# One fused kernel, one hand-written step list: the order of 808 steps is changed and 54 steps change engine

## The chip, the cores and the metric

The kernel runs on one core of one Trainium2 chip. The metric is the device time of one execution in microseconds (us). Five engines work side by side, each through its own list of instructions in order: TensorE (PE, matrix products into PSUM), VectorE (DVE), ScalarE (ACT), GpSimd (POOL), and SyncE (SP), which issues every DMA transfer of this kernel on one queue.

## The reference, cut to what matters

`x` is `A_q`, 2048 rows of 512 numbers in bf16.

```python
n  = layernorm(x)
ks = sum over t of shift(k, t) * shift_k[:, t]     # 4 taps
kv = ks * v
y  = causal_convolution(kv, ssm_k) + kv * ssm_D    # by FFT of length 4096
h  = x + n * y
m  = layernorm(h)
x1 = m + mixed(gelu(layernorm(m) @ w1)) @ w2       # four column groups shifted by +1, -1, +2, -2 rows
out = h + x1 + gelu(layernorm(x1) @ w3) @ w4       # w3: 512 x 1792, w4: 1792 x 512
```

## The kernel before, in words

The work is cut into 808 steps, each a small function that issues between none and some thirty instructions. `Plan.add` (line 71) numbers them; `Plan.emit` (line 80) walks the string `ORDER` (lines 31 to 63) and issues them in its sequence. A word such as `335P20` is step 335, on engine P (PE), with PSUM banks (or other buffer slots) 2 and 0. S is SP, V is DVE, A is ACT, G is POOL. Every engine therefore meets its steps in the sequence of this string, and waits where an input or a buffer slot isn't ready; whatever stands behind a waiting step on the same engine waits too. Costs in the source (such as `{V: 1.1, GP: 2.6}`) steer nothing at this point: the string decides.

The 2048 rows are two halves (s = 0, 1) of eight 128-row blocks b; a pair p is two neighbouring blocks. The stages:

- **Front** (about the first 64 us). Signals F0 and F1 are the two halves of the filter, A0 and A1 the two halves of `kv`. `K` (lines 433 to 445) makes four taps of `k` by matmuls against diagonal matrices `dg` (296), `KV` (447) multiplies by `v`. `S1`, `E1`, `X`, `S2`, `E2` (396 to 431) are the forward transform: PE product, evacuation of PSUM by ACT or DVE (`copy`, line 258), a re-ordering DMA of 256 KB (line 406), second product, second evacuation. `P` (474, DVE) multiplies spectra, `I2` (480, PE) transforms back, `EV` (492) evacuates, `XI` (495) re-orders by DMA, `I1` (499) ends the inverse. Tables of sines come from ACT; step `glu` (368) then loads ACT's table for GELU.
- **Head of each half.** `Q`, `QV`, `QP`, `QN` (506 to 542) are the statistics of the first normalisation, on eight blocks at once. `Y` (610) normalises a block into one of four slots `z`; `H` (617, DVE) adds the convolution and multiplies, and with it frees the PSUM bank of `I1` and the slot of `Y`; `HS` (623) is its statistics; `uw`, `rr`, `hn` (631 to 648) are small steps; `hb` (685) writes the normalised block; `LT` and `TE` (661 to 678) transpose it on PE with an evacuation, or by DMA for the pairs in `BYDMA` (659).
- **First product.** `W` (696, PE against w1) and `U` (704, GELU on ACT); `edge0`, `edge1`, `ed0`, `ed1` (575 to 578) fill boundary columns. `ed1` writes a region that the products `P` of half 1 read, so it waits for the last of them. `X2` (717, PE against w2), `S` (726), `SS` (735), `R` (730).
- **Second product.** `ux`, `r1`, `xn` (745 to 761), `lb` (763), `LX`, `EX` (transposes). `M` (774 to 787) is PE against w3, seven steps of eight matmuls (line 779) for a pair; `G` (788) is GELU on ACT; `O` (790 to 793) is PE against w4, fourteen matmuls (line 792); `Z` (794, DVE) adds, `OUT` (796) stores. The pairs come in the sequence of `PAIRS` (155); the pair (0,1) is the first, and its `M` begins while the front of half 1 is still under way.

The weights are loaded by one DMA each: `Lw1`, `Lw2` (571, 572; 512 KB), `Lw4` and `Lw3` (573, 574; 1792 KB). `Lw3` goes into the memory that held `k`. `Lw4` is first read by `O` of pair (0,1), `Lw3` by `M` of pair (0,1). On SP these loads stand among the eight transfers `X` of A1, of which the four with g = 0 wait for the last evacuation of A1, step `E1(A1,1,1)` on ACT.

Of the kernel before, what the change touches and what calls it, by code (L numbers as in the profile page):

```python
# [845 lines left out]
```

## Time and profile before

| | us |
|---|---|
| median of 3 runs | 214.28 |
| lowest, highest run | 213.77, 214.69 |
| the profiled execution: its own time | 214.16 |
| its span, first to last instruction | 212.4 |

So 1.8 us of the profiled execution lie around its span.

How to read it: section 1 of the page gives the busy time of each engine, section 2 the same in 40 slices of 5.3 us as digits in tenths. The chain is followed back from the last instruction. In a timeline row the first number is the start, the second the length, `xN` the number of instructions merged, and a bracket at the end is idle time of that engine ahead of the row, with what ended it. A row of SP is the issue of transfers, not their duration; the list of DMA issues gives the time from issue to landing.

| engine | busy us |
|---|---|
| PE | 196.5 |
| DVE | 145.6 |
| ACT | 126.4 |
| POOL | 73.7 |

### The profile page before, as it was taken

What the parts mean: (1) busy time and instruction counts of PE and PEld (TensorE: products, weight loads), DVE (VectorE), ACT (ScalarE), POOL (GpSimd) and SP (SyncE); (2) the same over time, 40 slices, a digit from 0 to 9 for tenths busy, and PEclk for the clock granted to TensorE, in tenths of its full rate; (3) what the DMA queues carried; (4) which work ended last, traced back from release to release, by engine and by line L of the source; (5) the groups of instructions that cost most, each with busy time, mean ns of one, the idle gap of its engine ahead of it and who ended that gap; (6) DMA issues with size and microseconds to landing.
All of it is one profiled execution on the core that took longest, in us unless ns stands there. A gap on an engine that the chain in (4) does not pass through costs nothing.

```text
span 212.4 us, 5087 instructions
## 1 busy us (share of the span) xinstructions
PE 196.5 (93%) x1962; PEld 118.2 (56%) x1980; DVE 145.6 (69%) x327; ACT 126.4 (59%) x206; POOL 73.7 (35%) x179
## 2 busy tenths in 40 slices
PE   5999957988779999999999999999999999999992
PEld 4454413443237656744854676666848578865540
DVE  6588999999999999999982984537578130004221
ACT  3639999979999978954660894446602415652100
POOL 8840106960888025520036664022806020000000
PEclk9999997999999999999999999999999999999999
DMA  6994899869786996024344016822043664001102
GB/s 196 332 403 178 329 365 292 238 158 289 302 219 270 341 385 229 4 49 102 98 103 127 26 37 140 149 49 49 5 112 110 149 77 99 0 3 52 46 0 74
DMA packets 30809, 32.86 MB, mean 155 GB/s; under 512 B 20545, under 2 KB 22594, under 8 KB 30530
## 3 DMA queue, kind: packets, MB, share of 16 engines
q1 hardware_dynamic: 30786, 32.55, 50.5%
q8 instruction: 15, 0.25, 0.5%
q14 instruction: 8, 0.07, 0.1%
HBM read 13.14 MB, written 4.46 MB: 83 GB/s over the span
## 4 chain that ended last, share of the span: by engine, by line
PE 69%; ACT 6%; issue 2%; DVE 0%; ACTq 0%; DVEq 0%
PE ps L779 23%; PE ps L792 23%; PE ps L701 7%; PE ps L724 6%; PE ps L485 4%; ACT r_z L258 2%; ACT r_a L258 2%; PE ps L503 2%; PE ps L414 2%; PE ps L672 1%; ACT junk L602 1%; PE ps L390 1%; ACT L368 1%; PE ps L443 0%; DVE r_v L794 0%
## 5 line engine op out<-in xcount | busy, mean ns | idle before, releaser
L779 PEld LDWEIGHTS <-r_k 128*128 128x128 bf16 x448 | 43.6, 98 | 7.6 <-issue 1.2
L794 DVE TENSOR_TENSOR r_v<-ps,r_v 128x512 bf16<-128x512 f32 x16 | 10.9, 688 | 40.8 <-PE ps L792 40.8
L475 DVE TENSOR_TENSOR r_p<-r_a,r_f 128x1024 bf16<-128x1024 bf16 x48 | 31.0, 702 | 0.0
L779 PE MATMUL ps<-r_dg,r_k 128*128 128x256 bf16 x224 | 25.8, 273 | 0.0
L258 ACT CAST r_a<-ps 128x1024 bf16<-128x1024 f32 x24 | 23.6, 1037 | 1.0 <-PE ps L414 0.7
L783 ACT ACTIVATE r_f<-ps 128x512 bf16<-128x512 f32 x14 | 7.6, 603 | 23.6 <-PE ps L779 23.5
L258 ACT CAST r_vs<-ps 128x1024 bf16<-128x1024 f32 x14 | 13.5, 1018 | 9.6 <-PE ps L485 8.7
L443 PE MATMUL ps<-r_dg,r_k 128*128 128x256 bf16 (+3 forms) x108 | 17.0, 308 | 1.7 <-DVE pb L323 1.4
L727 DVE SCALAR_TENSOR_TENSOR r_q<-r_v,hrr,ps 128x512 bf16<-128x512 bf16 x16 | 11.6, 740 | 8.0 <-PE ps L724 7.9
L485 PE MATMUL ps<-r_p,ttab 32*64 32x512 bf16 x384 | 15.0, 413 | 1.6 <-ACT r_a L258 0.8
L443 PEld LDWEIGHTS <-r_k 128*128 128x128 bf16 x112 | 10.0, 104 | 10.7 <-issue 6.1
L258 ACT CAST r_f<-ps 128x1024 bf16<-128x1024 f32 x14 | 13.4, 1042 | 4.1 <-PE ps L390 4.1
L615 POOL TENSOR_SCALAR z_t<-r_q,qrs,qnm 128x512 f32<-128x512 bf16 x13 | 11.7, 915 | 9.9 <-DVE r_v L618 9.7
L701 PEld LDWEIGHTS <-r_fx 128*128 128x128 bf16 x128 | 12.3, 98 | 2.4 <-issue 0.4
L750 POOL TENSOR_TENSOR xrr<-xrr,mhalf 128x2 f32<-128x2 f32 x8 | 5.9, 738 | 21.9 <-DVE xrr L747 21.5
L792 PE MATMUL ps<-w4s,r_a 128*128 128x512 bf16 x53 | 12.6, 379 | 0.2
L390 PEld LDWEIGHTS <-f 128*32 128x32 bf16 x256 | 6.6, 97 | 11.1 <-issue 6.9
L779 PE MATMUL ps<-xty,r_k 128*128 128x256 bf16 x112 | 12.7, 272 | 0.0
L779 PE MATMUL ps<-xtx,r_k 128*128 128x256 bf16 x112 | 12.7, 273 | 0.0
L792 PE MATMUL ps<-w4s,r_kv 128*128 128x512 bf16 x55 | 12.5, 379 | 0.1
L792 PE MATMUL ps<-w4s,r_v 128*128 128x512 bf16 x53 | 12.3, 379 | 0.3 <-issue 0.2
L451 DVE TENSOR_TENSOR r_kv<-ps,r_v 128x512 bf16<-128x512 f32 x16 | 10.4, 683 | 2.7 <-PE ps L443 2.6
(181 smaller groups left out, 359.1 us busy)
## 6 DMA issues: line engine op xcount, KB each, us to landing
r_z<-r_vs SPq DMA_DIRECT2D x16, 256.0 KB, 4.1
r_k<-in_kt_dram SPq DMA_DIRECT2D x8, 260.0 KB, 4.6
r_v<-in_v_dram SPq DMA_DIRECT2D x4, 512.0 KB, 6.1
r_q<-in_q_dram SPq DMA_DIRECT2D x8, 256.0 KB, 5.8
r_f<-r_f SPq DMA_DIRECT2D x8, 256.0 KB, 2.8
r_a<-r_a SPq DMA_DIRECT2D x8, 256.0 KB, 3.0
r_f<-r_a SPq DMA_DIRECT2D x8, 256.0 KB, 3.8
r_a<-r_z SPq DMA_DIRECT2D x8, 256.0 KB, 6.0
```

The costliest lines, as they stand in the source:

```text
L258: (act.copy if e in "AM" else on[e].tensor_copy)(o, i)
L443: nc.tensor.matmul(o[:, (d + j0) * P:(d + j1 + 1) * P], lhsT=kT[s][c][:, bb, x:x + P], rhs=diag[:, c, j0:j1 + 1, :].rearrange("p j x -> p ...
L451: vec.tensor_tensor(out=kvs[:, got(("K", g, 0), "kv")[0], :, c * P:(c + 1) * P], in0=ps[:, got(("K", g, c))[0], :].rearrange("p (b x) -> p ...
L475: on[e].tensor_tensor(out=prs[:, sl[0], :, :], in0=sp[a][:, kl, t, :, :], in1=gv, op=MUL)
L485: nc.tensor.matmul(ps[64 * t:64 * t + 64, bk[h], :], lhsT=ttab[32 * h:32 * h + 32, 2 * kl + t, 2 if x else xx, :], rhs=prs[32 * h:32 * h + ...
L615: on[e].tensor_scalar(out=z_t[:, sl[0], :], in0=qs, scalar1=qrs[:, i:i + 1], scalar2=qnm[:, i:i + 1], op0=MUL, op1=ADD)
L701: nc.tensor.matmul(ps[:, sl[0], j * 256:(j + 1) * 256], lhsT=w1s[:, k, m * P:(m + 1) * P], rhs=xt[:, k, :], start=(k == 0), stop=(k == DC ...
L724: nc.tensor.matmul(ps[:, sl[0], :], lhsT=h1T[s][:, m, bb, x:x + P], rhs=w2s[:, m, :], start=(m == 0), stop=(m == DC - 1))
L727: vec.scalar_tensor_tensor(out=q_sb[:, s, b, :], in0=h_sb[s][:, b, :], scalar=hrr[:, 4 * s + b // 2, 0, b % 2:b % 2 + 1], in1=ps[:, got((" ...
L779: nc.tensor.matmul(ps[:, sl[0], j * 256:(j + 1) * 256], lhsT=w3s[:, k, fc * P:(fc + 1) * P], rhs=xt[:, k, :], start=(k == 0), stop=(k == D ...
L792: nc.tensor.matmul(ps[:, sl[0], :], lhsT=gb[:, fc, (b % 2) * P:(b % 2 + 1) * P], rhs=w4s[:, fc, :], start=(fc == 0), stop=(fc == FC - 1))
L794: add(("Z", s, b), {V: 0.61}, lambda e, sl, b=b: vec.tensor_tensor(out=h_sb[s][:, b, :], in0=ps[:, got(("O", s, b))[0], :], in1=h_sb[s][:, ...
```

## The change

Only the string `ORDER` differs: the same 808 steps with the same functions, dependences and numbers of slots, in another sequence, with other slot numbers, and 54 of them on another engine.

| from, to | steps |
|---|---|
| ACT to DVE (15) | E1(A0,3,1), E2(F0,0,0), E2(A0,3,1), E1(F1,3,1), TE(0,4), EX(0,3), lb(0,0), EX(0,0), HS(1,3), TE(1,0), TE(1,1), SS(0,7), SS(1,2), SS(1,4), SS(1,7) |
| DVE to ACT (13) | E1(A0,0,0), E2(A0,3,0), E1(F1,0,0), E1(F1,1,1), TE(0,0), SS(0,4), EX(0,1), lb(0,5), HS(1,7), SS(1,3), lb(1,2), lb(1,4), SS(1,6) |
| POOL to DVE (9) | f2v, ux(0,2), Y(1,3), hb(1,4), ed0, lb(0,6), ux(1,2), lb(1,6), lb(1,1) |
| DVE to POOL (8) | lb(0,3), lb(0,1), QV(1), hb(1,2), ed1, xn(1,3), ux(1,0), lb(1,0) |
| POOL to ACT (6) | hb(0,4), Y(1,2), Y(1,0), Y(1,4), Y(1,6), lb(1,7) |
| ACT to POOL (3) | dg(2), Y(0,3), Y(1,5) |

The sequences on single engines at some places, read out of the string:

| engine, place | before | after |
|---|---|---|
| SP, first loads | Lk 0, Lk 3, Lf 3, Lk 2, Lv 0, Lf 2, Lv 1, Lf 1, Lk 1, Lsd, Lq 3, Lq 0, Lf 0 | Lk 0, Lf 3, Lk 2, Lsd, Lk 3, Lq 3, Lv 0, Lf 2, Lv 1, Lf 1, Lk 1, Lf 0, Lq 0 |
| SP, transfers of A1 | X 1,1; X 1,0; X 0,2; X 0,0; X 1,3; **Lw3**; X 0,1; X 0,3; **Lw4**; X 1,2 | X 1,3; X 1,0; X 0,2; X 0,0; X 1,1; X 1,2; X 0,3; **Lw4**; X 0,1; **Lw3** |
| ACT, end of F1 | four E1 of F1, glu, E1(F1,3,1), HS | six E1 of F1, HS (glu stands ahead of EV(0,2,0), behind E2(A0,3,0)) |
| POOL, head of half 1 | QP, QN, Y 3, 2, 0, 1, 4, 6 | ed1, QV, QP, QN, Y 1, 5 |
| ACT, head of half 1 | HS 0, HS 2, HS 1, Y 5, HS 3, HS 4, G(0,2) x3, hb(1,0), HS 5, TE(1,0), G x4 | Y 2, Y 0, Y 4, HS 1, HS 0, Y 6, HS 2, G x1, HS 5, HS 4, G x2, hb(1,0), HS 6, G x4 |
| PE, head of half 1 | I1 x4, M(0,2) x6, LT, LT, M(0,2), O(0,4) | I1 x3, M(0,2) x3, I1, M(0,2) x4, LT, LT, O(0,4) |
| PE, last pairs | M(1,1), O, O, M(1,3) x5, M(1,2), M(1,0) x6, O, then M and O in turn | M(1,1), M(1,2) x6, M(1,3), M(1,0) x6, M, O x3, M, O x5 |

Of the diff, the lines with the words of the loads (341 is Lw4, 342 is Lw3, 251 to 258 are X of A1), of `glu` (048), and of the head of half 1 (442 QV, 346 ed1, 445, 451, 454 and 460 Y, 335 to 338 I1):

```diff
...
-185P23 340S 184V 195P67 339S 186A 193P45 196V 189P01 194A 197P23 048A 190V 201S 198A 179P45 203S 180P67 359V 204S 181P01 362V 202S 360A 370G3 368V
...
-412P52 342S 415P6 407A 437V 393P7 252S 413A 422G 441V 416A 254S 391P4 217V 394A 341S 423G 417P5 392A 257S 218V 424G0 419P6 418A 427A3 259P2345 272V1
...
-654P2 328V6 329V7 321P45012 655A 440V 344G 324P 659A 442V 327P 330P 443G 332A 331V 661A 665P2 334S 444G 333S 454G2 451G0 662P6 666V 445G1 667S 448G3
-335P20 663V 336P14 664S 446V 337P57 447A 457G1 452V 338P62 449V 453A 455V 619P10 450A 463G3 458V 460A0 623P0 469G 456A 461V 621P4 459A 482V 470G 627P7
...
+160V0 154P 148S 159V1 225P2 155A 147S 162V2 012S 156A 163V3 136P4567 226V 231P3 137A 158S 138V 221P2 157S 048A 170V4 161P01452 232V 164P 169V5 233P3
...
+412P22 257S 216P6745 441V 407A 254S 415P3 422G 394A 413V 391P1 341S 218V 416A 252S 423G 419P0 392A 217V 342S 424G3 417P1 420A 272V1 427A0 425P03
...
+328V6 656P5 653A 609V 321P23671 329V7 657A 324P 655A 521V 327P 346G 330P 442G 662P1 332A 331V 333S 334S 443G 665P0 663V 664S 444G 448G1 451A3 445A0
+335P14 666V 336P56 454V2 446V 337P72 449V 457A0 619P30 452V 460G1 450A 455V 625P0 447A 461V 463A3 623P1 469G 456V 453A 338P62 624A 458V 470G 462A
...
```

54 lines of the change are left out of this document (27 added, 27 removed).

## Prediction

> **What bounds the kernel now.** First the page: busy times, then the slices.
>
> ```profile
> span 212.4 us, 5087 instructions
> PE 196.5 (93%) x1962; PEld 118.2 (56%) x1980; DVE 145.6 (69%) x327; ACT 126.4 (59%) x206; POOL 73.7 (35%) x179
> PE   5999957988779999999999999999999999999992
> DVE  6588999999999999999982984537578130004221
> PEclk9999997999999999999999999999999999999999
> ```
>
> PE is at 9 in every slice from the thirteenth (63.7 us) to the last but one. Before that it has holes. DVE is at 9 from about 21 to 106 us. So there are two stretches: a front in which evacuations and products on DVE and ACT set the pace, and from 64 us on a stretch in which PE never rests. The view of the stages and the list of waits say the same:
>
> ```profile
> 0.00:64.00 64.00, 52.82 (x691) 25.41 (x700) 57.36 (x117) 52.65 (x70) 32.83 (x98) 0.97 0.82 275
> 64.00:84.00 20.00, 19.89 (x263) 12.72 (x258) 19.82 (x41) 16.55 (x29) 8.13 (x26) 1.00 0.88 318
> 84.00:109.00 25.00, 24.77 (x348) 15.82 (x355) 24.83 (x47) 16.61 (x25) 5.16 (x9) 1.00 0.32 77
> 109.00:131.00 22.00, 21.89 (x171) 13.61 (x158) 15.19 (x58) 13.09 (x29) 14.36 (x25) 1.00 0.24 62
> 131.00:160.00 29.00, 28.74 (x184) 18.01 (x186) 15.48 (x45) 12.26 (x28) 8.62 (x19) 1.00 0.42 87
> 160.00:209.00 49.00, 48.41 (x332) 32.60 (x334) 12.54 (x24) 15.21 (x28) 4.63 (x4) 1.00 0.26 60
> PE ps L414 <- DMA r_a<-r_a: 2.0, 3, 0.8
> PE ps L390 <- ACT r_z L258: 1.9, 3, 1.2
> ```
>
> The columns are stretch, length, then busy us of PE, weight load, DVE, ACT, POOL, the granted clock, the DMA share and GB/s. In the waits the numbers are the total, how many, and the longest. From 64 to 209 us PE is idle for 1.3 us in all: 145.0 less 143.7, summing the five rows. PE's work is the same after the change, so this stretch can hardly become shorter; every late input in it makes it longer, one for one. The front has 11.2 us of PE idle time (64.00 less 52.82), but there DVE is busy for 57.4 us, and its step list begins late: what can be won there is small.
>
> **The change part by part.** I take the moves in order of time.
>
> **(1) The front.** Eight evacuations change sides, four from ACT to DVE and four back, so neither gains. `Y(0,3)` leaves ACT, `f2v` comes to DVE, and `glu` goes from the middle of the F1 evacuations to a place where ACT had idled:
>
> ```profile
> 43.86 0.82 ACT L613 ACTIVATE z_t<-r_q,qnm,qrs 128x512 f32<-128x512 bf16 x1
> 45.85 1.01 ACT L258 CAST r_vs<-ps 128x1024 bf16<-128x1024 f32 x1 [1.16 <-PE ps L485]
> 50.78 1.28 ACT L368 ACT_TABLE_LOAD   x1
> 52.07 0.20 ACT L368 ACTIVATE dum<-negpi 128x1 f32<-128x1 f32 x1
> 64.64 1.05 ACT L258 CAST r_z<-ps 128x1024 bf16<-128x1024 f32 x1
> ```
>
> The freed 0.82 and the idle 1.16 make room for the 1.28 + 0.20 of `glu`. Behind it ACT then saves 1.5 us, and pays one more evacuation in F1 (two in, one out, 1.0 us): 0.5 us earlier at the last evacuation of A1, the row at 64.64. DVE does `f2v`, two small instructions, in a place where it waits anyway. PE gets five more changes of tile shape ahead of 83 us, where it waits for evacuations in any case. I take -0.4 us; bounds -1.3 (the whole 1.5 + 0.8 less one evacuation of 1.0) and +1.0 (one evacuation more on the path).
>
> The first loads trade places within a few transfers of 256 KB; the k taps that PE takes first still come first. Cost 0, covered by PE's cold start; half a microsecond either way if not.
>
> **(2) The load of w3.** This is the term that decides. SP's issues and their landings, then PE at the place where w3 is first read:
>
> ```profile
> 66.31 2.23 SPq L406 DMA_DIRECT2D r_a<-r_z  x3
> 68.59 0.59 SPq L267 DMA_DIRECT2D r_k<-in_w_dram  x1
> 69.22 1.17 SPq L406 DMA_DIRECT2D r_a<-r_z  x2
> 70.44 0.58 SPq L267 DMA_DIRECT2D w4s<-in_w_dram  x1
> r_k<-in_w_dram SPq DMA_DIRECT2D x1, 1792.0 KB, 9.2
> w4s<-in_w_dram SPq DMA_DIRECT2D x1, 1792.0 KB, 13.8
> r_a<-r_z SPq DMA_DIRECT2D x1, 256.0 KB, 14.2
> 83.13 3.65 PE L779 MATMUL ps<-r_dg,r_k 128*128 128x256 bf16 x32
> 67.30:84.30 17.00, 16.89 (x219) 10.88 (x219) 16.86 (x36) 13.87 (x25) 5.61 (x18) 1.00 0.91 324
> 75.00:80.00 5.00, 4.95 (x95) 2.63 (x95) 4.96 (x12) 3.54 (x8) 1.69 (x6) 1.00 0.99 412
> ```
>
> Now w3 (into `r_k`) is issued at 68.59 and lands 9.2 us later, at 77.8; w4 lands at 70.44 + 13.8 = 84.2; the last transfer of A1, issued at 71.07, lands 14.2 us later, at 85.3. The first `M`, line 779, reads w3 at 83.13: 5.3 us of slack. The queue is full all that time (share 0.91). After the change the same bytes go through the same queue behind the same release (the last evacuation of A1, which ends at 64.64 + 1.05 = 65.7): six transfers of 256 KB and two of 1792 KB, but w3 is now the last of them. So it lands when the last now lands, 84.2 to 85.3. PE wants it at 83.13: a wait of 1.1 to 2.2 us, and nothing can go ahead of it, since PE keeps its order. I take 1.6. Below, the bound is 0: at the best row's 412 GB/s the 5.1 MB (6 x 256 + 2 x 1792 KB) take 12.5 us from 67.3, and would be through at 79.8. Above, 2.2. w4 is then early, which is worth nothing: its first reader comes after `M`. With the front's -0.4 the first `M` starts about 1.2 us later than now.
>
> [...]
>
> **(3) DVE up to the last product of half 1.** From 64 to 109 us DVE is full. Counting the steps ahead of the last `P`: seven leave it (TE(0,0), lb(0,3), lb(0,1), lb(0,5), EX(0,1), SS(0,4), R(0,0)), seven come (TE(0,4), EX(0,3), EX(0,0), lb(0,0), ux(0,2), Q(1,6), Z(0,3)), of one size: copies and normalisations against copies and normalisations, one statistics each, a residual against a sum,
>
> ```profile
> L731 DVE SCALAR_TENSOR_TENSOR r_v<-r_q,hnm,r_v 128x512 bf16<-128x512 bf16 x16 | 11.6, 743 | 0.1
> L794 DVE TENSOR_TENSOR r_v<-ps,r_v 128x512 bf16<-128x512 f32 x16 | 10.9, 688 | 40.8 <-PE ps L792 40.8
> ```
>
> with 743 ns against 688. So 0, and the first `M` being late gives PE's need another 1.2 us of slack. Bounds 0 and +0.5.
>
> **(4) The head of half 1.** In the kernel before, ACT and POOL here:
>
> ```profile
> 109.82 1.64 POOL L530 TENSOR_TENSOR qrs<-qsd,mhalf 128x8 f32<-128x8 f32 x1 [9.15 <-DVE qsd L525]
> 112.30 3.02 POOL L615 TENSOR_SCALAR z_t<-r_q,qrs,qnm 128x512 f32<-128x512 bf16 x4
> 117.44 0.63 ACT L602 ACTIVATE junk<-r_v 128x512 bf16<-128x512 bf16 x1 [6.05 <-DVE r_v L618]
> 119.57 0.80 ACT L613 ACTIVATE z_t<-r_q,qnm,qrs 128x512 f32<-128x512 bf16 x1
> 121.99 1.57 ACT L783 ACTIVATE r_kv<-ps 128x512 bf16<-128x512 f32 x3 [0.25 <-PE ps L779]
> 33.84 0.58 POOL L515 TENSOR_TENSOR qnm<-qst 128x8 f32<-128x8 f32 x1 [9.49 <-DVE qst L507]
> 38.14 0.52 POOL L525 TENSOR_SCALAR qsd<-qsd 128x8 f32<-128x8 f32 x1
> 111.54 0.20 POOL L536 TENSOR_TENSOR qsd<-qsd,qrs 128x8 f32<-128x8 f32 x1
> 123.02 0.54 DVE L615 TENSOR_SCALAR z_t<-r_q,qrs,qnm 128x512 f32<-128x512 bf16 x1
> ```
>
> ACT idles for 6.05 us up to 117.44, and then has no hole over 0.25 us until after 128: it is as late as it may be. Of the four `Y` that come to ACT two fit into the 6 us, two (0.80 each) stand behind `H` steps in the full part; one `Y` leaves: +0.8 us there. `Y(1,3)` on DVE puts 0.54 us ahead of `H(1,0)`. The last `I1` must now wait for `H(1,3)` and `H(1,5)`, whose banks it takes, and the GELUs that `O(0,4)` reads stand behind `hb(1,0)` and an `HS`. Together 1.3 us of delay against the present slack of some 0.4: +0.9. Bounds: 0 (if the later start of `M` has given all of it back) and +2.0. `QV(1)` on POOL waits behind `ed1`, that is for the last `P`. Its eight small instructions cost 0.2 us each when DVE lets POOL alone (row 111.54), with gaps an estimated 2.3 in all, or 4.8 as in the front (33.84 to 38.66). DVE then is done with its products, so I take 2.3, and the statistics are ready before PE's `I1`, which come 1.2 us later than now: 0.
>
> [...]
>
> **(5) The last pairs.** PE's sequence M(1,1), M(1,2), M(1,3), M(1,0) now follows the DMA transposes' order. The `R` and `Z` steps crowd on DVE ahead of `Z(0,6)`, and `lb(1,7)` stands on ACT ahead of the first GELU of pair (1,1): the sixth and seventh `M` of that pair can miss a bank. +0.3 us, bounds 0 and +1.0. The changes of tile shape from the first `M` on are ten in both orders, and the tail (one `Z`, one store) is the same: 0.
>
> **The sum.** -0.4 + 1.6 + 0 + 0.9 + 0.3 = +2.4 us on the profiled execution's 214.16: 216.6. That execution is 0.1 us below the median, which I leave aside.
>
> **The rivals.** *First, not slower: the front wins.* If ACT's last evacuation of A1 comes 1.3 us earlier and the queue runs faster than now, w3 is there when PE asks, and the head of half 1 fits into the slack. Time 212.9, or with w3 still 1.3 us behind the wish, 214.5; I set 213.9. For it: `glu` stands in the chain now. Against it: DVE's 57.4 of 64 us. The point where it turns is the last evacuation of A1: it must start before 63.3 and w3 must land within 18.4 us of that start, where now the last landing comes 20.7 us after (85.3 less 64.64). Chance 0.18.
>
> *Second: the head of half 1 is dear.* `QV(1)` takes 4.8 us, `H(1,0)` is 1 us later and the last `I1` misses its banks by as much; with it the upper bound of term 4, and the time 214.16 - 0.4 + 1.6 + 2.0 + 1.0 = 218.4. For it: the row at 33.84. Against: POOL's neighbours there are no products. Chance 0.15.
>
> *Third: the clock falls.* The row below has 0.57 of the clock over four microseconds in which PE was merely holed:
>
> ```profile
> 34.00:38.00 4.00, 3.49 (x64) 1.65 (x63) 4.00 (x8) 3.80 (x5) 3.92 (x7) 0.57 0.96 300
> ```
>
> That is 1.7 us lost (0.43 x 4). It came in the front among waits for DMAs of 0.8 us at most (the row of line 414); a wait of 1.6 amid shape changes at 83 us could do it again, where PE has no slack: 216.6 + 1.7 = 218.3. Against it: after the 1.2 us wait for ACT (line 390) the clock stayed at 9. Chance 0.07.
>
> **How the numbers follow.** The forecast, 215.4 to 218.1, has 0.58; the rivals 0.18, 0.15 and 0.07; 0.02 is for anything longer. About 0.5%, 1.1 us, is what a measurement of this kernel tells from no change: below 213.2 is faster, above 215.4 slower. Faster needs the first rival's better end: 0.05. The same gets the rest of that rival, 0.13, and 0.04 of the forecast's lower edge: 0.17. Slower 0.78. The range of 214.0 to 219.0 leaves out about 0.1 on each side; adding all upper bounds would give more than 220, but they share slack.
>
> **What would show it.** A wait of PE ahead of line 779 at 83 to 85 us, ended by the DMA into `r_k`, of 1 to 2 us, with w3 landing behind w4. ACT without holes from 118 to 130 us and a hole on PE at lines 672 or 792 there. PE full otherwise. I am wrong if w3 lands before 83 us, if the front ends more than 1 us earlier or later, or if PE has new holes after 140 us of over 1 us.

## The result, and the profile after

Over 21 runs of each on the same chips the kernel before takes 213.81 us (median; 213.38 to 215.22), the kernel after the change 215.25 us (213.89 to 216.58). The ratio is 1.0062, 95% interval 1.0044 to 1.0080: slower by 1.3 us (0.9 to 1.7), where I had forecast +2.4 on the profiled execution. The profiled execution of after takes 215.13 us with a span of 213.4, which is 1.0 us more than that of before in both. The direction was right; the size, and the place where I looked for it, were not. The ratios here and below leave out runs that are more than 1.5% above the fastest of their kernel (two of the eighth, one of the eighteenth); the medians have them.

First the page of after, with the rows that stood first in the prediction: busy times, then the 40 slices.

```profile
span 213.4 us, 5081 instructions
PE 196.6 (92%) x1964; PEld 117.0 (55%) x1980; DVE 144.7 (68%) x330; ACT 126.5 (59%) x203; POOL 74.8 (35%) x183
PE   5969948998789999999999999999999999999992
PEclk9999995999999999999999999999999999999999
```

The picture is the same: holes in PE up to about 64 us, none behind. The clock has one deep slice, the seventh (32 to 37 us), where before had a shallow one. Now the stages, in the same stretches and columns as in the prediction:

```profile
0.00:64.00 64.00, 52.19 (x680) 23.55 (x684) 55.03 (x116) 49.95 (x64) 31.25 (x92) 0.95 0.84 278
64.00:84.00 20.00, 19.54 (x254) 12.56 (x264) 19.86 (x42) 16.92 (x29) 9.69 (x31) 1.00 0.85 320
84.00:109.00 25.00, 24.79 (x330) 16.16 (x340) 23.98 (x47) 17.44 (x27) 9.02 (x13) 1.00 0.30 73
109.00:131.00 22.00, 21.83 (x195) 13.44 (x183) 15.41 (x54) 13.62 (x29) 13.58 (x27) 1.00 0.22 57
131.00:160.00 29.00, 28.79 (x188) 18.16 (x188) 21.22 (x56) 12.61 (x25) 7.67 (x12) 1.00 0.42 87
160.00:209.00 49.00, 48.84 (x336) 33.03 (x338) 8.46 (x20) 15.96 (x31) 3.58 (x10) 1.00 0.23 60
```

From 84 us on PE is as full as before: 0.75 us idle in the four rows (24.79 + 21.83 + 28.79 + 48.84 = 124.25 of 125), against 1.19 in before. So the head of half 1 and the last pairs have cost nothing in this execution. That stretch even gains a little: from the start of the first `M` (in the rows below) to the end it takes 130.66 us (215.13 - 84.47), in before 131.03 (214.16 - 83.13). The list of PE's waits from 84 us to the end has one entry, and it is no wait for another engine:

```profile
PE ps L792 <- issue: 0.2, 1, 0.2
```

The loss is there before 84 us. The rows of PE around the first `M` (line 779), which in before started at 83.13, and the issues and the landing of w4 and w3:

```profile
83.92 0.63 PE L414 MATMUL ps<-r_a,ftab 64*32 64x512 bf16 x16
84.47 1.70 PE L779 MATMUL ps<-r_dg,r_k 128*128 128x256 bf16 x14
```
```profile
70.43 0.59 SPq L267 DMA_DIRECT2D w4s<-in_w_dram  x1
71.63 0.69 SPq L267 DMA_DIRECT2D r_k<-in_w_dram  x1
```
```profile
r_k<-in_w_dram SPq DMA_DIRECT2D x1, 1792.0 KB, 12.6
```

w3 is issued last and lands at 71.63 + 12.6 = 84.2 us, where I had it (84.2 to 85.3). But PE arrives at 84.47 without a bracket: no wait. The first `M` is 1.34 us later than before because PE itself comes later. Where does that begin? PE's rows for the second product of A0, where before had a bracket of 0.75, and SP's issues of the re-ordering transfers (line 406) ahead of it, `r_f<-r_f` for F0 and `r_a<-r_a` for A0. After:

```profile
27.36 1.29 PE L414 MATMUL ps<-r_f,ftab 64*32 64x512 bf16 x32 [0.51 <-DVE qst L507]
30.38 0.62 PE L414 MATMUL ps<-r_a,ftab 64*32 64x512 bf16 x16 [1.73 <-DMA r_a<-r_a]
```
```profile
19.92 5.17 SPq L406 DMA_DIRECT2D r_f<-r_f  x8
25.20 1.83 SPq L406 DMA_DIRECT2D r_a<-r_a  x3
```

and before:

```profile
19.77 3.90 SPq L406 DMA_DIRECT2D r_f<-r_f  x6
24.75 1.73 SPq L406 DMA_DIRECT2D r_a<-r_a  x2
26.53 0.60 SPq L406 DMA_DIRECT2D r_f<-r_f  x1
29.10 0.81 PE L414 MATMUL ps<-r_a,ftab 64*32 64x512 bf16 x16 [0.75 <-DMA r_a<-r_a]
```

The order before puts six transfers of F0 ahead of the first two of A0, and lets the last two of F0 follow. The changed order puts all eight ahead. PE's sequence is F0, F0, F0, A0, F0, A0, A0 in both, so the fourth product now waits 1.73 us instead of 0.75 and starts at 30.38 instead of 29.10. The sequence within F0 differs too. PE's first product of F0 needs two transfers that were the first and second of the queue and are now the second and fifth; the next two are complete at places 7 and 8 instead of 4 and 6. My prediction doesn't speak of these sixteen words at all.

### The profile page after: what moved, and what is told of

Its sections match the earlier page's. It is cut to its first block, busy times and chain, and to the rows that moved or that the text cites. A ratio compares the mean times of both kernels' runs of the same rounds, so it can differ in the third digit from the quotient of the medians.

```text
span 213.4 us, 5081 instructions
## 1 busy us (share of the span) xinstructions
PE 196.6 (92%) x1964; PEld 117.0 (55%) x1980; DVE 144.7 (68%) x330; ACT 126.5 (59%) x203; POOL 74.8 (35%) x183
## 4 chain that ended last, share of the span: by engine, by line
PE 62%; ACT 11%; DMA 9%; DVE 8%; issue 4%; SPq 4%; POOL 1%; DVEq 0%; ACTq 0%; POOLq 0%
PE ps L792 22%; PE ps L779 20%; PE ps L485 5%; PE ps L724 4%; DMA r_k<-in_kt_dram 4%; ACT r_a L258 4%; PE ps L701 3%; PE ps L443 3%; DMA r_f<-r_a 2%; DVE r_f L426 2%; PE ps L414 2%; SPq L267 2%; PE ps L390 2%; DVE r_p L475 2%; ACT junk L602 2%
## 5 line engine op out<-in xcount | busy, mean ns | idle before, releaser
L475 DVE TENSOR_TENSOR r_p<-r_a,r_f 128x1024 bf16<-128x1024 bf16 x48 | 30.1, 683 | 0.1
L258 ACT CAST r_a<-ps 128x1024 bf16<-128x1024 f32 x25 | 24.5, 1043 | 2.6 <-PE ps L414 2.4
L779 PE MATMUL ps<-r_dg,r_k 128*128 128x256 bf16 x224 | 25.3, 273 | 0.0
L443 PE MATMUL ps<-r_dg,r_k 128*128 128x256 bf16 (+3 forms) x109 | 16.2, 296 | 2.1 <-DVE pb L323 1.4
L258 ACT CAST r_f<-ps 128x1024 bf16<-128x1024 f32 x13 | 12.6, 1016 | 8.0 <-PE ps L390 7.3
L783 ACT ACTIVATE r_a<-ps 128x512 bf16<-128x512 f32 x14 | 7.5, 600 | 14.8 <-PE ps L779 14.8
L485 PE MATMUL ps<-r_p,ttab 32*64 32x512 bf16 x384 | 14.5, 408 | 0.2 <-ACT r_a L258 0.2
L615 POOL TENSOR_SCALAR z_t<-r_q,qrs,qnm 128x512 f32<-128x512 bf16 x10 | 9.7, 981 | 12.4 <-DVE r_v L618 12.2
L701 PEld LDWEIGHTS <-r_fx 128*128 128x128 bf16 x128 | 12.5, 98 | 2.1
L507 DVE BATCH_NORM_STATS2 qst<-r_q 128x6 f32<-128x512 bf16 x16 | 10.6, 678 | 3.9 <-DMA r_q<-in_q_dram 3.9
L515 POOL TENSOR_TENSOR qnm<-qst 128x8 f32<-128x8 f32 x2 | 4.8, 2377 | 24.2 <-DVE qst L507 24.2
L390 PEld LDWEIGHTS <-f 128*32 128x32 bf16 x256 | 6.2, 97 | 12.7 <-issue 7.2
L779 PE MATMUL ps<-xtx,r_k 128*128 128x256 bf16 x112 | 12.7, 272 | 0.0
L792 PE MATMUL ps<-w4s,r_kv 128*128 128x512 bf16 x55 | 12.5, 379 | 0.1
L792 PE MATMUL ps<-w4s,r_v 128*128 128x512 bf16 x53 | 12.3, 379 | 0.3 <-issue 0.2
```

What stands on the lines that cost most here:

```text
L258: (act.copy if e in "AM" else on[e].tensor_copy)(o, i)
L390: nc.tensor.matmul(ps[32 * j:32 * j + 32, sl[hh], :], lhsT=tab[:, 4 * t + 2 * hp + hh, :], rhs=src(2 * b + b0), start=(i == 0), stop=(i == ...
L443: nc.tensor.matmul(o[:, (d + j0) * P:(d + j1 + 1) * P], lhsT=kT[s][c][:, bb, x:x + P], rhs=diag[:, c, j0:j1 + 1, :].rearrange("p j x -> p ...
L475: on[e].tensor_tensor(out=prs[:, sl[0], :, :], in0=sp[a][:, kl, t, :, :], in1=gv, op=MUL)
L485: nc.tensor.matmul(ps[64 * t:64 * t + 64, bk[h], :], lhsT=ttab[32 * h:32 * h + 32, 2 * kl + t, 2 if x else xx, :], rhs=prs[32 * h:32 * h + ...
L507: return lambda e, sl: vec.bn_stats(qst[:, 8 * s + b, :], q_sb[:, s, b, :])
```

## The experiments

**Theory 1**, from these rows: the transfers of F0 and A0 delay the front by about 1.2 us; w3's late landing is a second delay that ends at the same place, the first `M`; the later one counts, so the two do not add. **Theory 2**: w3's place does nothing. **Theory 3**: w3's place is the whole cause. Each kernel is measured against the kernel before on the same chip. "before" and "after" in the diffs are the two orders; a join of two orders is shown by the line at the join, with the slot numbers renamed so that both halves fit.

| | kernel | median us | ratio to before | 95% interval |
|---|---|---|---|---|
| 1 | before, w3 last | 215.39 | 1.0075 | 1.0045 to 1.0105 |
| 2 | after, w3 ahead of w4 | 215.02 | 1.0045 | 1.0026 to 1.0064 |
| 3 | after to the first M, then before | 216.49 | 1.0109 | 1.0090 to 1.0128 |
| 4 | before with w3 last to the first M, then after | 216.80 | 1.0129 | 1.0111 to 1.0146 |
| 5 | after to X2 of block 1, then before | 216.33 | 1.0101 | 1.0073 to 1.0129 |
| 6 | before to X2 of block 1, then after | 214.30 | 1.0009 | 0.9994 to 1.0024 |
| 7 | after to the first I1, then before | 216.00 | 1.0089 | 1.0068 to 1.0110 |
| 8 | before, after from I1 to X2, before | 215.08 | 1.0023 | 0.9996 to 1.0051 |
| 9 | after to 35 us, then before | 215.44 | 1.0049 | 1.0028 to 1.0070 |
| 10 | before to 35 us, then after | 214.14 | 0.9996 | 0.9979 to 1.0013 |
| 11 | before, first loads of after | 214.32 | 1.0011 | 0.9981 to 1.0041 |
| 12 | before, transfers of F0 and A0 of after | 215.11 | 1.0052 | 1.0023 to 1.0081 |
| 13 | after, two transfers put back | 214.80 | 1.0029 | 1.0006 to 1.0053 |
| 14 | 13 with w3 ahead of w4 | 214.63 | 1.0018 | 0.9995 to 1.0041 |
| 15 | 10 with one exchange of H | 214.42 | 1.0000 | 0.9980 to 1.0020 |
| 16 | after, once more | 215.30 | 1.0051 | 1.0026 to 1.0076 |
| 17 | before, 1 and 12 together | 216.52 | 1.0113 | 1.0082 to 1.0144 |
| 18 | 1 once more | 215.30 | 1.0050 | 1.0019 to 1.0080 |

In 1, 4, 13, 16, 17 and 18 w3 is last in the queue, in the others it stands ahead of w4. A difference of 0.001 in the ratio is 0.21 us.

**1, w3 last.** One word moved, behind the last transfer of A1:

```diff
-412P52 342S 415P6 407A 437V 393P7 252S 413A 422G 441V 416A 254S 391P4 217V 394A 341S 423G 417P5 392A 257S 218V 424G0 419P6 418A 427A3 259P2345 272V1
+412P52 415P6 407A 437V 393P7 252S 413A 422G 441V 416A 254S 391P4 217V 394A 341S 423G 417P5 392A 257S 342S 218V 424G0 419P6 418A 427A3 259P2345 272V1
```

> The kernel before with one word moved: the load of w3 goes behind the last transfer of A1, so that it is last in the queue as after the change. Everything else as before. Theory 1 (the front and the load of w3 are two delays that overlap, and the later one counts): w3 lands at 84.2 to 85.5 us, PE waits for it at the first M (line 779) for 1.0 to 2.0 us, and the time is +1.2 us against before (+0.6 to +1.8). Theory 2 (the order of w3 does nothing, only the front counts): 0, within 0.4 us. Theory 3 (the order of w3 is the whole cause): +1.4.

It is slower by 1.6 us (1.0 to 2.2), so theory 2 falls. In its profiled execution, which at 214.52 us is well below the median of 215.39, PE waits half a microsecond, with the bracket that I had forecast:

```profile
83.45 3.67 PE L779 MATMUL ps<-r_dg,r_k 128*128 128x256 bf16 x32 [0.49 <-DMA r_k<-in_w_dram]
```

No execution of the median's length was profiled, so the rows account for half a microsecond of the 1.6 only.

**2, the opposite in the kernel after.**

```diff
-412P22 257S 216P6745 441V 407A 254S 415P3 422G 394A 413V 391P1 341S 218V 416A 252S 423G 419P0 392A 217V 342S 424G3 417P1 420A 272V1 427A0 425P03
+412P22 257S 216P6745 441V 407A 254S 415P3 422G 394A 413V 391P1 342S 218V 416A 252S 423G 419P0 392A 217V 341S 424G3 417P1 420A 272V1 427A0 425P03
```

> The kernel after with the loads of w3 and w4 exchanged, so that w3 stands ahead of w4 as before. Theory 1: the front alone already makes the first M start at 84.3 to 84.6, so the time stays within 0.4 us of after, +1.2 against before (+0.8 to +1.6). Theory 2: the same, +1.3. Theory 3: the time of before, 0 within 0.4.

1.0 us slower than before: theory 3 falls. Inside the changed kernel w3's place is worth 0.1 to 0.4 us (0.0045 against 0.0051 and 0.0062, with intervals that overlap, so that it can't be told from 0), not 1.6.

**3 and 4, front and rest exchanged at the first `M`.** Step 591 is the first `M`:

```diff
 3
-262P0123 539V 591P70 264A 640G 438V 601P4 263A 535V 641G 593P5 645G3 540V 536A 287V0 592A 265P2301 602A 288V1 599P6 594A 611V 267A 595P7 291V2 612G
+262P0123 539V 435V 439V 591P50 535V 264A 536V 595P0 263A 640G 533V 603P4 592A 641G 596A 593P2 540V 604A 642A0 265P6701 645V3 288V0 601P3 594A 529V
 4
-262P6723 591P10 535V 264A 639G 536V 595P4 263A 640G 533V 603P0 592A 539V 641G 596A 593P2 540V 604A 642A0 265P6745 645V3 288V0 601P3 594A 529V 611G
+262P6723 285S 639G 440V 539V 591P50 264A 640G 438V 601P6 263A 535V 641G 593P7 645G3 540V 536A 287V0 592A 265P2301 602A 288V1 599P4 594A 611V 267A
```

> All words of the order after the change ahead of the first M, with w3 ahead of w4, then the rest of the order before (PSUM banks renamed where the two meet). The front is that of after, the queue order of w3 and everything from 83 us on are those of before. Theory 1: first M at 84.2 to 84.6, time +1.2 against before (+0.8 to +1.6). Theory 2: +1.3. Theory 3: 0 within 0.4.

> The reverse: all words of before ahead of the first M, with w3 last in the queue, then the rest of the order after the change. Theory 1: PE comes to the first M at 83.1 and waits 1.0 to 2.0 us for w3, time +1.2 against before (+0.6 to +1.8), so no better than after although the front is better. Theory 2: 0 within 0.4. Theory 3: +1.4. If the head of half 1 or the last pairs cost anything of their own (my steps 4 and 5), the time is more than that of the first kernel, by their price.

Both are slower than I expected, and the join is to blame for a part that I can't separate: in the fourth kernel the first `M` waits for a sum on DVE that frees its PSUM bank, since steps of DVE stand in another sequence ahead of it.

```profile
84.98 1.91 PE L779 MATMUL ps<-r_dg,r_k 128*128 128x256 bf16 x16 [1.76 <-DVE r_q L727]
87.98 0.27 PE L779 MATMUL ps<-r_dg,r_k 128*128 128x256 bf16 x1 [1.10 <-ACT r_a L258]
```

These 1.76 and 1.10 us belong to neither order. Nothing is concluded from these two.

**5 to 8, joins where both orders have issued the same steps.** Step 522 is `X2` of block 1, 179 the first `I1`:

```diff
 5
-215V 276P 582G 279P 282P 214V 583G 522P2 284A 584V 518P3 585G2 283A 523V 286S 534P6 588G1 524A 519V 285S 586P70 520V 589P4 538P5 587A 590V 639G 440V
+215V 276P 582G 279P 282P 214V 583G 522P6 284A 584V 518P7 588V2 283A 435V 585G1 534P2 523V 586P30 439V 286S 524A 589P0 538P1 519V 587A 590A 520V
 6
-214V 276P 582G 279P 282P 215V 583G 522P2 284A 584V 518P3 588V1 283A 435V 585G2 534P0 523V 586P10 439V 286S 524A 589P4 538P5 519V 587A 590A 520V
+214V 276P 582G 279P 282P 215V 583G 522P0 284A 584V 518P1 585G1 283A 523V 286S 534P2 588G2 524A 519V 285S 586P30 520V 589P6 538P7 587A 590V 639G 440V
 7
-367G2 197P23 194A 196V 364G3 189P67 190A 183P01 198V 185P45 184A 205S 186A 204S 179P67 340S 180P23 203S 362V 200S 181P01 359V 363A 373G0 199S 368V
+367G2 197P23 194A 196V 364G3 189P67 190A 183P01 198V 185P45 184A 205S 186A 204S 340S 201S 179P67 203S 180P23 359V 181P01 362V 202S 360A 370G0 368V
 8
-185P23 340S 184V 195P67 339S 186A 193P45 196V 189P01 194A 197P23 048A 190V 201S 198A 179P45 203S 180P67 359V 204S 181P01 362V 202S 360A 370G3 368V
+185P23 340S 184V 195P67 339S 186A 193P45 196V 189P01 194A 197P23 048A 190V 201S 198A 205S 204S 179P45 180P67 203S 362V 200S 181P01 359V 363A 373G3
```

> The two orders have issued exactly the same steps when PE comes to X2 of block 1 (78.5 us in before). Here the order is that of after up to this step, with w3 ahead of w4, and that of before from it on; the join is at a better place than in the second hybrid of the first four, whose first M waited 0.5 us for a sum on DVE. Theory 1 (front and w3 are two delays that overlap): the front's delay alone, +1.2 us against before (+0.9 to +1.6). The theory that w3's place is the whole cause: 0 within 0.4.

> The reverse: before up to X2 of block 1, with w3 early as it is there, then after. If all of the loss is in the front and the place of w3, and what follows 80 us is free or a small gain (PE's lead of before over after shrank from 1.4 us at the first M to 1.0 at the end): -0.3 us against before (-0.7 to +0.1). If the head of half 1 or the last pairs cost what I had forecast (+0.9 and +0.3): +1.0.

> After up to the first I1 of half 0 (52 us), then before. Theory: most of the front's delay arises here (first loads, the order of the re-ordering transfers of F0 and A0, the products with KV between them), so first I1 at 51.9 to 52.3, and the time +0.9 us against before (+0.5 to +1.2). If DVE's order of H were the main cause: 0 to +0.3.

> Before up to the first I1 of half 0, then after with w3 early up to X2 of block 1, then before. Theory: only the 0.4 us that DVE waits because H of block 1, which needs the second half of the first I1, stands ahead of H of block 0: +0.4 us against before (0 to +0.7). If the middle is the main cause: +1.2.

The sixth kernel is the answer on everything from 78 us on, the head of half 1 and the last pairs among it: +0.2 us (-0.1 to +0.5), where my steps 4 and 5 say +1.2. It includes what its join costs: in its profiled execution 131.5 us lie behind the start of the first `M`, in that of after 130.66. The fifth has all of the loss and more (+2.2 us, 1.6 to 2.8), the seventh +1.9. In the seventh a part may again be the join: the product of F1 waits 1.75 us for its transfers, and the longest such wait in after is 0.4 us, in before none is listed.

```profile
60.83 0.94 PE L414 MATMUL ps<-r_f,ftab 64*32 64x512 bf16 x16 [1.75 <-DMA r_f<-r_a]
```

The eighth is +0.5 us (-0.1 to +1.1; +1.0 by the medians), as expected for the exchange of `H`, and cannot be told from 0. So most of the loss starts ahead of the first `I1`; a cost of the middle of up to a microsecond is not excluded.

**9 and 10, a join at 35 us.** Step 153 is the last product `P` ahead of the join:

```diff
 9
-130P4523 126S 350V 086A 014S 349V 011S 131A 133P0167 139V1 355G 143V2 132A 142V3 135A 141P45230 149V4 144P 150V5 134A 153V6 146A 151P67011 152V7 145A
+130P4523 126S 350V 086A 014S 349V 011S 131A 133P0167 139V1 355G 143V2 132A 142V3 135A 141P45230 149V4 144P 150V5 134A 012S 153V6 152V7 146A 151P01671
 10
-139V1 017S 085A 018S 143V2 131A 011S 133P0167 352V 122S 142V3 132A 355G 013S 149V4 014S 134A 141P45230 150V5 144P 153V6 135A 152V7 146A 151P01671
+139V1 017S 085A 018S 143V2 131A 011S 133P0167 352V 122S 142V3 132A 355G 013S 149V4 014S 134A 141P45230 150V5 144P 339S 135A 153V6 146A 151P67011 152V7
```

> After up to the product P for tap group 1 of half 0 (35 us, where both orders have issued the same steps but for one load), then before. Theory A: the front's delay is made ahead of 35 us (first loads, Q of block 6 on DVE waiting for its block, all transfers of F0 ahead of those of A0, the clock at half for longer): +1.2 us against before (+0.8 to +1.9). Theory B: it is made between 35 and 52 us, where DVE meets KV behind P and ACT the step glu ahead of two evacuations: 0 within 0.4.

> The reverse, before up to the same place, then after with w3 ahead of w4. Theory A: +0.3 us against before (0 to +0.6), since only the middle's 0.4 us is left and what comes after 80 us gives a little back. Theory B: +1.0, the time of after with w3 early.

Theory A holds: after up to 35 us costs 1.0 us (0.6 to 1.5), and after from 35 us on, with w3 early, costs nothing (-0.1; -0.4 to +0.3). So `glu` and the sequence of `KV` and `P` behind 35 us cost nothing on balance; a cost of some 0.4 us there could hide behind the 0.4 us that the changed order gains from the first `M` on.

**11 and 12, one part of the first 35 us alone.** First the loads (two lines of SP's words), then the sixteen transfers (four lines, of which two are shown):

```diff
 11
-005S 029P0 008S 004S 007S 009S 003S 033V 010S 030P 031V 037V 002S 095P10 006S 036G 000S 024S 063P23 343G 038G 021S 065P45 035A 001S 087P01 020S 039G
+005S 029P0 004S 007S 000S 008S 024S 033V 009S 030P 031V 037V 003S 095P10 010S 036G 002S 006S 063P23 343G 038G 001S 065P45 035A 021S 087P01 016S 039G
...
 12
-117P23 116A 105P01 067S 046V 219P61 040V 073S 118A 350V 069S 113P45 047A 106V 041A 227P70 050G 220V 114A 078P2301 119S 349V 229P6 079A 123S 228V 070S
-080A 230V 075P4523 351V 077A 081P6701 074S 348V 120S 076A 082V 124S 083A 127P2345 354V 121S 128V 129A 125S 084P6701 126S 086A 140V0 130P4523 012S
+117P23 116A 105P01 069S 046V 219P61 040V 068S 118A 350V 070S 113P45 047A 106V 041A 227P70 050G 220V 114A 078P2301 067S 349V 229P6 079A 073S 228V 123S
+080A 230V 075P4523 351V 077A 081P6701 119S 348V 121S 076A 082V 120S 083A 127P2345 354V 124S 128V 129A 125S 084P6701 122S 086A 140V0 130P4523 012S
...
```

> Before with nothing but its first nineteen loads in the sequence of after (SP's words exchanged among their own places). If the first loads are the cause: +0.8 us or more. I expect +0.2 (-0.2 to +0.6), since PE's first matmuls come no later in the trace of after.

> Before with nothing but the sixteen re-ordering transfers of F0 and A0 in the sequence of after, all of F0 ahead of A0. In the trace of after PE waited 1.7 us for the first of A0 at 30 us. If that wait carries through: +1.0 us (+0.6 to +1.4). If DVE sets the pace of the front and the wait is absorbed: 0 within 0.4.

The loads give +0.2 us (-0.4 to +0.9). The transfers alone give +1.1 us (0.5 to 1.7), as much as all of after up to 35 us, and the bracket is that of after:

```profile
19.55 5.17 SPq L406 DMA_DIRECT2D r_f<-r_f  x8
25.44 3.20 SPq L406 DMA_DIRECT2D r_a<-r_a  x3
```
```profile
30.60 1.05 PE L414 MATMUL ps<-r_a,ftab 64*32 64x512 bf16 x16 [1.65 <-DMA r_a<-r_a]
```

The delay carries through. In this execution the last evacuation of A1 on ACT starts at 65.53 us (64.64 in before), and the first `M` 0.89 us later than in before as well:

```profile
84.02 3.65 PE L779 MATMUL ps<-r_dg,r_k 128*128 128x256 bf16 x32
```

The other profiled executions point the same way. In the nine with all of F0 first, those of after among them, the fourth product starts at 28.7 to 30.6 us (mean 29.8), in the eleven with two of A0 ahead of the last two of F0 at 27.4 to 30.0 (mean 28.3). So the sequence of the sixteen transfers is shown to be a cause, and the only one of this size found in the front. How much of it is A0 behind F0, and how much the sequence within F0, this kernel does not separate.

**13 to 16, after with the causes taken out.** Words 070 and 074 (F0, kl = 3) go behind 119 (the second of A0); in the fourteenth 341 and 342 change places too, as in 2. The fifteenth is 10 with `H` of block 0 (359) ahead of block 1 (362) again. The sixteenth is after itself.

```diff
 13
-089P6 058A 032V 092V 059P23 090V 051P45 049G 060A 348V 097P0 354V 052A 061P67 098V 053P23 062A 352V 103P45 105P01 054V 104A 074S 115P67 072S 116A 106V
-107P45 071S 111P23 108A 113P67 069S 040V 117P01 068S 114A 112V 219P40 070S 041A 109P67 067S 118V 227P51 073S 110A 220V 123S 351V 119S 078P2301 228V
+089P6 058A 032V 092V 059P23 090V 051P45 049G 060A 348V 097P0 354V 052A 061P67 098V 053P23 062A 352V 103P45 105P01 054V 104A 115P67 072S 116A 106V
+107P45 071S 111P23 108A 113P67 069S 040V 117P01 068S 114A 112V 219P40 041A 109P67 067S 118V 227P51 073S 110A 220V 123S 351V 119S 070S 074S 078P2301
...
 15
-367G2 197P23 194A 196V 364G3 189P67 190A 183P01 198V 185P45 184A 205S 186A 204S 179P67 340S 180P23 203S 362V 200S 181P01 359V 363A 373G0 199S 368V
+367G2 197P23 194A 196V 364G3 189P67 190A 183P01 198V 185P45 184A 205S 186A 204S 179P67 340S 180P23 203S 359V 200S 181P01 362V 363A 373G0 199S 368V
```

> After with two words moved: the transfers of F0 for kl = 3 go behind the first two of A0, as before has them. w3 stays last in the queue. Theory 1 (two delays, the later one counts): S2 of A0 starts at 29.0 to 29.6 us and the front's delay is gone, but now the first M waits for w3, by 0.5 to 1.5 us; the time is +0.9 us against before (+0.4 to +1.5). Theory 2 (w3's place does nothing, the transfers are all): 0 within 0.4.

> The same with w3 ahead of w4 as well. Theory 1: both delays are gone; 0 us against before (-0.4 to +0.5; the middle's 0.4 us is left, and what comes after 80 us gives some back). If there is a third cause of more than half a microsecond in the order after the change: +0.6 or more.

> The best version that the parts suggest: before up to 35 us, then after with w3 ahead of w4, and H of block 0 ahead of H of block 1 again. Without this last exchange the time was that of before. If the exchange costs 0.4 us on the path: -0.4 us against before (-0.8 to 0).

> The changed kernel itself, in the same call as its two mended versions: +1.3 us against before (+0.8 to +1.8).

With two words put back the loss goes from 1.1 to 0.6 us (0.1 to 1.1), and with w3 early to 0.4 (-0.1 to +0.9), which can't be told from 0. The intervals overlap with that of the sixteenth (0.6 to 1.6), so the half microsecond of the two words alone isn't clear of noise. The profiles are mixed too: the fourth product starts at 28.48 us in the thirteenth kernel, behind a wait of 0.70, but at 30.01 in the fourteenth, behind one of 1.47. The exchange of `H` is worth nothing (0.0, -0.4 to +0.4), so no version beats the kernel before. The sixteenth kernel brought what I had not looked for. It is the changed kernel, word for word, and in this execution the front was faster, with the fourth product at 28.67 us and the last evacuation of A1 at 64.37:

```profile
82.35 0.63 PE L414 MATMUL ps<-r_a,ftab 64*32 64x512 bf16 x16
84.38 1.81 PE L779 MATMUL ps<-r_dg,r_k 128*128 128x256 bf16 x15 [1.40 <-DMA r_k<-in_w_dram]
```
```profile
70.92 0.58 SPq L267 DMA_DIRECT2D r_k<-in_w_dram  x1
```
```profile
r_k<-in_w_dram SPq DMA_DIRECT2D x1, 1792.0 KB, 13.4
```

Here PE waits 1.40 us for w3, the wait of my second step, and the first `M` starts at 84.38, not at 84.47. Two executions of one kernel, the same start of `M`, two different reasons.

**17 and 18, do the two delays overlap or add?** The edits of 1 and 12 together on the kernel before, and 1 once more:

```diff
 17
-117P23 116A 105P01 067S 046V 219P61 040V 073S 118A 350V 069S 113P45 047A 106V 041A 227P70 050G 220V 114A 078P2301 119S 349V 229P6 079A 123S 228V 070S
+117P23 116A 105P01 069S 046V 219P61 040V 068S 118A 350V 070S 113P45 047A 106V 041A 227P70 050G 220V 114A 078P2301 067S 349V 229P6 079A 073S 228V 123S
...
-412P52 342S 415P6 407A 437V 393P7 252S 413A 422G 441V 416A 254S 391P4 217V 394A 341S 423G 417P5 392A 257S 218V 424G0 419P6 418A 427A3 259P2345 272V1
+412P52 415P6 407A 437V 393P7 252S 413A 422G 441V 416A 254S 391P4 217V 394A 341S 423G 417P5 392A 257S 342S 218V 424G0 419P6 418A 427A3 259P2345 272V1
```

> Before with exactly two edits, each of which was run alone: the sixteen transfers of F0 and A0 in the sequence of after (+1.0 us alone), and w3 last in the queue (+1.5 us alone). Theory 1 (both delays end at the same place, the first M, and the later one counts): +1.6 us against before (+1.1 to +2.0). If the two add, as my forecast added its terms: +2.5 us (+2.1 or more).

> The kernel with w3 last alone once more, in the same call as the one with both edits: +1.5 us against before (+0.9 to +1.9), if the first measurement of it (+1.0 to +2.2) was no chance. If the place of w3 costs less than half a microsecond: 0 to +0.5.

In the kernel before they add: +2.4 us (1.8 to 3.1), as 1.1 for the transfers and 1.3 for w3 (the mean of its 1.6 and 1.1) give. So theory 1 falls there, for the larger of the two alone is 1.3, though the lower end of 1.8 is still inside the range that I had given it. In the changed kernel they don't: there w3 last costs only 0.1 to 0.4 us more than the transfers alone (kernel 2). The rows of the seventeenth kernel, and beside them those of the eighteenth:

```profile
71.52 0.58 SPq L267 DMA_DIRECT2D r_k<-in_w_dram  x1
```
```profile
r_k<-in_w_dram SPq DMA_DIRECT2D x1, 1792.0 KB, 13.9
```
```profile
82.77 0.63 PE L414 MATMUL ps<-r_a,ftab 64*32 64x512 bf16 x16
85.50 0.72 PE L779 MATMUL ps<-r_dg,r_k 128*128 128x256 bf16 x5 [2.11 <-DMA r_k<-in_w_dram]
```
```profile
70.77 0.58 SPq L267 DMA_DIRECT2D r_k<-in_w_dram  x1
```
```profile
r_k<-in_w_dram SPq DMA_DIRECT2D x1, 1792.0 KB, 12.5
```
```profile
83.33 2.90 PE L779 MATMUL ps<-r_dg,r_k 128*128 128x256 bf16 x25 [0.30 <-DMA r_k<-in_w_dram]
```

w3 stands behind the last transfer of A1, which waits for the end of the front. So a late front can make PE late and w3's issue late alike; that this is why they add is argued, not shown, for in the seventeenth kernel w3 is issued 0.75 us later than in the eighteenth, and the other 1.4 us are a slower landing (13.9 against 12.5). PE would come to the first `M` 11.9 us after w3's issue in the seventeenth kernel (85.50 - 2.11 - 71.52), 12.3 in the eighteenth (83.33 - 0.30 - 70.77), 12.1 in the sixteenth (84.38 - 1.40 - 70.92), 12.7 in the first (83.45 - 0.49 - 70.22), and came 12.8 after it in the profiled execution of after (84.47 - 71.63). w3 lands 12.5 to 13.9 us after its issue, and the wait is the difference, to 0.1 us: 2.1, 0.3, 1.4, 0.5 and 0.

## Why the prediction was wrong

**(1) The front, -0.4 forecast: the step whose mechanism failed.** The front costs about +1.1 us when its cause stands alone. I took the front from the evacuations that change sides and from the place of `glu`, and "the first loads trade places", and left the sixteen transfers of F0 and A0 out, though PE's largest wait in the list of before was the one for `DMA r_a<-r_a`, 2.0 us. The row was quoted and not followed to the words on SP. The +1.1 (0.5 to 1.7) lies at the edge of my bounds (-1.3 to +1.0), which were drawn for another cause. What I did price shows no cost or gain of its own: the first loads, which I took to be covered by PE's slow start (a product of line 443 with 384 columns takes 524 ns up to 8 us and 326 from 12 to 20 us in the profile of before), give +0.2 (kernel 11), the moves behind 35 us, `glu` among them, -0.1 (kernel 10), and all moves ahead of 35 us together no more than the transfers alone (kernel 9, 1.0, against kernel 12, 1.1).

**(2) w3, +1.6 forecast: the mechanism was right, the size holds for the kernel before and failed in the changed one.** Alone it costs 1.3 us (two measurements, 1.6 and 1.1), PE's bracket is the one that I named, and w3's landing in after, 84.2 us, is the lower of my two figures. In the changed kernel it is worth only 0.1 to 0.4 us (kernel 2 against after and 16, kernel 14 against 13). In the profiled execution of after PE comes to the first `M` late, counted from w3's issue (12.8 us), and the landing was a quick one (12.6), so there was no wait. But neither belongs to the changed order alone: kernel 1, with the sequence of before, has 12.7, kernel 18 a landing of 12.5, and kernel 16, the changed order, has 12.1 and 13.4. So why w3 is worth so little in the changed kernel stays open.

**(3) DVE to the last product, 0 forecast.** DVE is busy for 19.86 and 23.98 us in the rows 64 to 84 and 84 to 109, 0.8 less than before, and kernel 6 finds no cost.

**(4) The head of half 1, +0.9 forecast: wrong, and with step 2 the reason that the sum is too large.** Kernel 6 gives +0.2 (-0.1 to +0.5) for this and all that follows, kernel 10 -0.1. ACT is without holes from 118.8 us, as I said, and yet PE waits for nobody: the slack was larger than the 0.4 us that I gave it. The statistics of half 1 on POOL were dearer than my 2.3, and dearer than the 4.8 of my second rival: 6.6 us from the start of the first row to the end of the last.

```profile
104.46 4.18 POOL L515 TENSOR_TENSOR qnm<-qst 128x8 f32<-128x8 f32 x1 [8.33 <-DVE qst L507]
108.61 0.20 POOL L516 TENSOR_TENSOR qrs<-qst 128x8 f32<-128x8 f32 x1
109.10 0.74 POOL L519 TENSOR_SCALAR qmv<-qnm 128x8 f32<-128x8 f32 x1
110.88 0.20 POOL L525 TENSOR_SCALAR qsd<-qsd 128x8 f32<-128x8 f32 x1
```
```profile
118.81 0.81 ACT L613 ACTIVATE z_t<-r_q,qnm,qrs 128x512 f32<-128x512 bf16 x1 [3.72 <-DVE r_v L618]
```

They also started earlier than I had thought, for `ed1` did not wait for the last `P`, as I had it here and in the description of the kernel: it ran at 95.91 us, and the last `P` starts at 109.10. And at 118.81 the normalisation on ACT, which reads them, waits for DVE and not for POOL. So the price was above both my figures and still hidden.

**(5) The last pairs, +0.3 forecast.** Nothing, by the same two kernels.

**The sum.** Forecast -0.4 + 1.6 + 0 + 0.9 + 0.3; the runs put +1.1 (alone) or +0.5 (in after) for the first term, +1.3 (alone) or some 0.3 (in after) for the second, 0 for the others. By the figures for after the forecast was too high by 1.3 at w3, 0.9 at the head and 0.3 at the last pairs, and too low by 0.9 or more at the front. That the direction came out right is in part luck: I had put the loss on w3 and the head, and the term with the largest measured price in the changed kernel is one that I had forecast as a gain. What stays open: in the kernel before the two causes together cost 2.4 us, the changed kernel has both and loses 1.1 to 1.3. Something in the rest of the changed order gives back about 1 us. Some 0.4 of it stand in the profiles: from the first `M` to the end it takes 130.65 to 130.68 us in after and in kernels 2, 10, 13, 14 and 15, which all have the changed order there, and 131.03 to 131.13 in before and in kernels 1, 8, 9, 11, 12 and 18, which have the order of before (the sixteenth, at 131.07, and the seventeenth, at 130.78, don't fit; both wait over 1 us for w3). The interval of kernel 10 (-0.4 to +0.3) has room for such a gain. The rest I could not find. The granted clock is not it: its mean is 0.979 over the runs of after and 0.984 over those of kernel 16, and 0.986 over those of kernel 17, which loses more.

**The rivals and the signs.** The front did not win. The head of half 1 was not dear. The clock did not fall at 83 us, where the third rival had it (1.00 from 64 us on in the rows of after). In the front it fell for longer in the profiled execution of after (0.95 of the clock up to 64 us, against 0.97), but kernel 12 loses its 1.1 us at the mean clock of before, 0.981 in both. Of my three signs of being wrong one came: by ACT's last evacuation of A1 the front ends 1.04 us later (65.68 against 64.64). w3 did not land before 83 us, and PE has no new holes behind 140 us.

## What to carry to other kernels

When a hand-written order changes, compare each queue's sequence against the sequence of its consumer, every queue, and begin with the wait that is the longest in the list of before: a transfer that moves ahead of the one that is wanted next can hold up its consumer, and here a new sequence of sixteen transfers cost 1.1 us of the whole. If a load stands behind something that the critical path also waits for, don't count on the path's lateness to cover that of the load: in the kernel before the two added to 2.4 us, in the changed one they did not. One profiled execution shows one draw: two profiles of the same kernel showed a wait of 0 and of 1.4 us at the same instruction, so a cause is settled by leaving it out and timing, not by the bracket.

## What the runs showed of the hardware

The 4.18 us of the POOL row above are about the length of a stretch on DVE, 4.29 us. DVE's rows at that place, in after:

```profile
104.29 4.29 DVE L475 TENSOR_TENSOR r_p<-r_a,r_f 128x1024 bf16<-128x1024 bf16 x7
108.50 0.68 DVE L794 TENSOR_TENSOR r_v<-ps,r_v 128x512 bf16<-128x512 f32 x1
109.10 0.68 DVE L475 TENSOR_TENSOR r_p<-r_a,r_f 128x1024 bf16<-128x1024 bf16 x1
```

An instruction of POOL on 128 x 8 numbers starts 0.17 us after the first of seven products with two inputs from SBUF and ends when the last of them ends (108.64 and 108.58). The next one, beside an instruction of DVE that takes an input from PSUM, has 0.20 us; the one at 109.10 has 0.74, beside a product of 0.68. In this stretch, from 104.29 to 108.58, POOL ends no instruction and begins only this one. In the front of the kernel before it ends and begins more. There DVE has nine such products without a pause,

```profile
33.67 5.54 DVE L475 TENSOR_TENSOR r_p<-r_a,r_f 128x1024 bf16<-128x1024 bf16 x9
```

and the eight small instructions of POOL that lie beside them from 33.84 to 38.66 us take 0.52 to 0.65 us each. What decides between the two is open. So neither the 0.2 us that I took for such an instruction nor the 4.8 us for all eight can be carried from one place of a kernel to another.

The time from issue to landing of one and the same load behind the same transfers varies by 1.4 us between executions: 12.5 to 13.9 us for the 1792 KB of w3, in the rows of kernels 18 and 17 above.

The granted clock falls in the front, and the longest wait of PE between 20 and 42 us is 0.8 us in before and 1.7 us in after. In the profiled execution of before it is 0.50 from 34.5 to 37.9 us, in that of after 0.50 from 31.6 to 38.4 us. Between 31 and 42 us this gives 0.69 in after and 0.84 in before (the eighth column):

```profile
31.00:42.00 11.00, 9.19 (x141) 3.35 (x126) 10.84 (x17) 10.70 (x12) 7.26 (x13) 0.69 0.82 257
```
```profile
31.00:42.00 11.00, 8.91 (x158) 4.12 (x160) 10.69 (x18) 10.42 (x12) 7.64 (x13) 0.84 0.89 279
```

Over the runs of kernel 8 the mean clock goes from 0.966 to 1.000, and two with 1.000 took 212.72 and 213.38 us, where the median is 215.08. The other runs with 1.000 lie closer to the median of their kernel: 1.1 us below it in before (213.18) and in kernel 9 (214.34), 0.5 to 0.7 in kernels 12, 16 and 17. So an estimate from these seven runs is that an order which keeps PE from such falls would be worth 0.5 to 2.4 us. That the clock makes these runs short, and isn't only found with them, was not tested, nor which order would do it.
